# First batch of a Fourier-filter and MLP kernel: whole filter rows, units of four frequencies, the sign in the product, and three quarters of the last stages moved into the MLP

## The chip, the cores and the metric

The kernel runs on one core of one Trainium2 chip. The metric is the device time of one execution in microseconds (us). The kernel before takes 785.2 us (median of 3 runs, 785.15 to 785.42). Executions have two states, fast and slow.

Engines are named as the profile names them: PE is TensorE (matmuls), PEld its weight loads, DVE is VectorE, ACT is ScalarE, POOL is GpSimd, SP is SyncE (it issues transfers). L433 is line 433 of that kernel's file.

## The reference

```python
# x: 8 x 3008 x 256, filt_r and filt_i: 1505 x 256, w_in: 256 x 2048, w_out: 2048 x 256, beta: 2048
X = np.fft.rfft(x, axis=1)
y = np.fft.irfft(X * (filt_r + 1j * filt_i)[None], n=3008, axis=1)
h = y.reshape(24064, 256) @ w_in
g = h * (1.0 / (1.0 + np.exp(-beta * h)))
out = g @ w_out
```

## The kernel before

The Fourier filter is done as four matmul stages per batch element ("batch" below): stages 1 and 2 transform (3008 = 47 x 64), then comes the product with the filter, and stages 3 and 4 transform back. The MLP then runs over 47 blocks of 512 tokens in 16 steps each, 752 steps in all. A step is two matmuls into `hps`, one Silu on ScalarE from `hps` into `gT`, and four matmuls into `acc`.

Batch 0 is filtered before the MLP starts (the "setup"). Batches 1 to 7 are filtered inside the MLP, their instructions dealt out to its steps by a plan. The setup handles its product in six *units*. A unit is 8 of the 24 frequency groups and half of the 256 columns, so that a product on VectorE is 128x1024:

```python
parts = ((0, KH, 0, E2), (KH, 2 * KH, 0, E2), ...)      # KH = 8, E2 = 128: half rows, 512 bytes
def load_filters(k0, k1, d0, d1):
    for filt, dst, p0 in ((filt_r, fr_sb, 0), (filt_i, fi_sb, M)):        # M = 64
        for q0, off, sg in ((p0, k0, 1), (p0 + H, N1 - k0, -1)):          # H = 32 partitions each
            ...
            nc.sync.dma_start(dst[q0 : q0 + H, k0:k1, d0:d1], src)

def s2_0(n):                                   # stage 2 and the filter product of one unit
    ...
    for c, filt in enumerate((fr_sb, fi_sb)):
        r_t = p0pool.tile([P, KH, P], BF16, name="pq_t", tag=f"pq{c}")
        nc.vector.tensor_tensor(r_t[:], ps[:], filt[:, ks, ds], ALU.mult)

def spread(n):                                 # the second copy of the filter, in the other 64 partitions
    ...
    nc.gpsimd.tensor_copy(fr_sb[M:, ks, ds], fr_sb[:M, ks, ds])
    nc.gpsimd.tensor_copy(fi_sb[:M, ks, ds], fi_sb[M:, ks, ds])

# order on GpSimd: spread 0 to 4, load of w_in (1 MB), spread 5, loads of batch 1
```

Stage 3 used two tables, `t3` and a rotated copy `t3s` that carried the sign of the complex product. After it, TensorE turned (transposed) the result in 64 pieces (`z_turn`), stage 4 followed (`f_0`, `s4_0`), and all of that was done before the MLP. In the MLP the plan places the units of batch 1:

```python
s1_steps(1, range(16), [o + i // 2 for i in range(16)], False, range(1, 16, 2))
s23_steps(1, [o + r for r in (19, 21, 23, 26, 28, 30, 34, 36, 39, 41, 44, 46)], 5, 1)
```

A finished block leaves `acc` through two copies on VectorE into `ost`, queued two steps into the next block. `acc` has three buffers, and a block takes two.

## Time and profile before

| what | value | view |
|---|---|---|
| span of the profiled run | 782.8 us | head of the page |
| TensorE busy | 764.2 us, 98% | busy time by engine |
| TensorE busy from 60 to 120 us | 19.84 to 19.89 of each 20 us | busy time by stretches |
| first MLP matmul | 41.54 us | timeline of TensorE |
| products of the setup | 12, 1.14 us apart, 16.54 to 32.76 us | timeline of VectorE |

The busy time by engine on the page of the kernel before:

```profile
PE 764.2 (98%) x5978; PEld 544.9 (70%) x6071; DVE 438.1 (56%) x682; ACT 558.5 (71%) x824; POOL 151.6 (19%) x160
```

Busy time by stretches, kernel before (columns: stretch, its length, then busy time and instruction count of each engine, granted TensorE clock, DMA share, GB/s):

```profile
60.00:80.00 20.00, 19.89 (x144) 14.16 (x146) 16.83 (x25) 15.98 (x27) 9.55 (x10) 1.00 0.60 126
80.00:100.00 20.00, 19.84 (x140) 13.81 (x141) 13.22 (x20) 16.20 (x27) 7.62 (x6) 1.00 0.55 142
100.00:120.00 20.00, 19.84 (x159) 13.58 (x161) 11.81 (x19) 13.99 (x23) 1.54 (x3) 1.00 0.83 210
```

TensorE is the bound once the MLP runs. The setup is not bound by it: between 30 and 42 us it has gaps. Timeline of the kernel before (columns: start, duration, engine, line, operation, output<-inputs, shapes, and in brackets the idle time before it and what ended it), three lines of VectorE, then two of GpSimd and two of TensorE:

```profile
16.54 1.23 DVE L433 TENSOR_TENSOR pq_t<-sps,fr_sb 128x1024 bf16<-128x1024 f32 x1 [0.75 <-POOL fi_sb L468]
17.68 1.22 DVE L433 TENSOR_TENSOR pq_t<-sps,fi_sb 128x1024 bf16<-128x1024 f32 x1
...
31.55 1.21 DVE L433 TENSOR_TENSOR pq_t<-sps,fi_sb 128x1024 bf16<-128x1024 f32 x1
...
13.76 1.04 POOL L467 COPY fr_sb<-fr_sb 64x1024 f32<-64x1024 f32 x1 [3.18 <-DMA fr_sb<-in_filt_r_dram]
14.92 1.14 POOL L468 COPY fi_sb<-fi_sb 64x1024 f32<-64x1024 f32 x1
...
41.54 0.38 PE L756 MATMUL hps<-y,win_sb 128*128 128x512 bf16 x1 [0.43 <-ACT y L112]
42.30 0.39 PE L756 MATMUL hps<-y,win_sb 128*128 128x512 bf16 x1 [0.38 <-DVE y L116]
```

A unit of filter costs GpSimd two copies of about 1.04 us, and VectorE two products 1.14 us apart. GpSimd is thus as fast as VectorE. The transfers, kernel before, from 13 to 26 us (filter rows of 512 bytes), then from 26 to 28 us (the w_out loads, rows of 1 KB). The line that starts with q1 gives a queue's packets, MB, and the time that its packets took, as a share of 16 engines' time:

```profile
DMA packets 5817, 2.93 MB, mean 226 GB/s; under 512 B 336, under 2 KB 5816, under 8 KB 5816
...
DMA packets 665, 0.68 MB, mean 338 GB/s; under 512 B 15, under 2 KB 664, under 8 KB 664
...
q1 hardware_dynamic: 664, 0.66, 106.7%
```

### The profile page before, as it was taken

The page shows a single profiled execution, that of the slowest core. Times are in us where ns is not written, and L with a number is a line of the kernel's source. Part 1 is how long each engine was busy: PE and PEld are TensorE (multiplying, and loading weights), DVE is VectorE, ACT ScalarE, POOL GpSimd, SP SyncE. Part 2 cuts the span into 40 slices and gives each one's busy share as a digit, 9 for nine tenths or more (in the row PEclk, how much of TensorE's full clock was granted, in tenths as well). Part 3 has the DMA queues.
Part 4 walks back from the last instruction along what each step waited for, and adds up shares of the span by engine and source line. Part 5 has one row for each costly group of instructions (what it writes and reads, how often), then busy time and mean ns, then how long its engine had stood idle before and what let it go on. Part 6 is the DMA issues. An engine that isn't in the chain of part 4 may idle for free.

```text
span 782.8 us, 15166 instructions
## 1 busy us (share of the span) xinstructions
PE 764.2 (98%) x5978; PEld 544.9 (70%) x6071; DVE 438.1 (56%) x682; ACT 558.5 (71%) x824; POOL 151.6 (19%) x160
## 2 busy tenths in 40 slices
PE   8799999999999999999999999999999999999997
PEld 5666767766677667866678666786667776676665
DVE  7747654776556665566655675466655666320101
ACT  6788867676667766776667776677666777777776
POOL 6714300322012120122101222012200222000000
PEclk9999999999999999999999999999999999999999
DMA  9966675234822349033580416612164211500101
GB/s 178 230 190 138 145 201 167 68 88 120 238 75 64 98 114 260 32 84 99 121 236 29 126 56 158 198 58 85 49 188 118 66 48 49 155 28 28 55 28 55
DMA packets 89835, 88.51 MB, mean 113 GB/s; under 512 B 5708, under 2 KB 80972, under 8 KB 89764
## 3 DMA queue, kind: packets, MB, share of 16 engines
q1 hardware_dynamic: 85588, 73.81, 31.8%
q0 software_dynamic: 4032, 13.60, 10.5%
q8 instruction: 47, 0.77, 0.4%
q14 instruction: 24, 0.20, 0.1%
q10 hardware_dynamic: 144, 0.13, 0.1%
HBM read 54.47 MB, written 46.66 MB: 129 GB/s over the span
## 4 chain that ended last, share of the span: by engine, by line
PE 94%; ACT 2%; issue 1%; DVE 0%; ACTq 0%
PE acc L774 43%; PE hps L756 39%; PE ps L572 3%; PE ps L639 3%; PE ps L617 3%; PE ps L588 2%; ACT zT L112 1%; ACT zz L112 1%; ACT t3s L291 0%; DVE y L116 0%; PE sps L396 0%; PE sps L444 0%; PE tps L396 0%; ACT a L112 0%; PE sps L428 0%
## 5 line engine op out<-in xcount | busy, mean ns | idle before, releaser
L765 ACT ACTIVATE gT<-hps,beta_sb 128x512 bf16<-128x512 f32 x752 | 515.8, 687 | 208.3 <-PE hps L756 187.2
L774 PE MATMUL acc<-wout_sb,gT 128*128 128x256 bf16 x3008 | 453.2, 272 | 2.5
L756 PE MATMUL hps<-y,win_sb 128*128 128x512 bf16 (+7 forms) x1636 | 428.3, 350 | 1.1 <-ACT y L112 0.6
L774 PEld LDWEIGHTS <-gT 128*128 128x128 bf16 x3008 | 287.6, 98 | 125.9 <-issue 1.2
L607 POOL TENSOR_TENSOR yh<-a_t,b_t 128x512 bf16<-128x512 f32 x84 | 106.4, 1266 | 420.4 <-DVE b_t L606 419.5
L756 PEld LDWEIGHTS <-win_sb 128*128 128x128 bf16 x1728 | 164.9, 98 | 25.6 <-issue 0.7
L114 DVE COPY ost<-acc 128x512 f32<-128x512 f32 (+1 forms) x94 | 60.0, 679 | 147.1 <-PE acc L774 147.1
L114 DVE CAST a<-ps 96x512 bf16<-96x512 f32 x104 | 70.9, 685 | 52.1 <-PE ps L572 48.0
L602 DVE TENSOR_TENSOR a_t<-ps,fr_sb 128x512 f32<-128x512 f32 x84 | 58.1, 692 | 70.0 <-PE ps L588 69.5
L116 DVE TENSOR_SCALAR y<-ps 128x376 bf16<-128x376 f32 x104 | 56.0, 548 | 59.3 <-PE ps L639 59.1
L603 DVE SCALAR_TENSOR_TENSOR b_t<-ps,fi_sb 64x512 f32<-64x512 f32 x84 | 58.2, 692 | 1.1
L606 DVE TENSOR_TENSOR b_t<-ps,fi_sb 64x512 f32<-64x512 f32 x84 | 57.4, 683 | 1.1
L114 DVE CAST z<-ps 128x512 bf16<-128x512 f32 x72 | 49.3, 684 | 1.7 <-PE ps L617 0.8
L639 PEld LDWEIGHTS <-zz 96*128 96x128 bf16 x448 | 29.8, 98 | 22.9
L572 PE MATMUL ps<-xg,t 94*96 94x512 bf16 x112 | 41.5, 381 | 0.6
L639 PE MATMUL ps<-t,zz 96*128 96x94 bf16 x448 | 34.7, 205 | 0.8
L617 PE MATMUL ps<-yh,t 128*128 128x256 bf16 x168 | 32.1, 273 | 0.6
L588 PE MATMUL ps<-a,t 128*128 128x256 bf16 x168 | 32.1, 273 | 0.3
L617 PEld LDWEIGHTS <-t 128*128 128x128 bf16 x168 | 16.3, 98 | 17.7
L588 PEld LDWEIGHTS <-t 128*128 128x128 bf16 x168 | 16.1, 98 | 15.2
L171 POOL DMA_DIRECT2D xg<-in_x_dram x24 | 12.4, 519 | 56.5 <-PE ps L572 56.5
L572 PEld LDWEIGHTS <-t 94*96 94x96 bf16 x112 | 13.8, 123 | 10.3
(103 smaller groups left out, 185.9 us busy)
## 6 DMA issues: line engine op xcount, KB each, us to landing
out_dram<-ost SPq DMA_DIRECT2D x46, 512.0 KB, 3.0
d<-a SPq DMA_DIRECT2D x28, 384.0 KB, 4.7
a<-d SPq DMA_DIRECT2D x28, 384.0 KB, 5.1
d<-z SPq DMA_DIRECT2D x28, 384.0 KB, 3.7
zz<-d SPq DMA_DIRECT2D x28, 384.0 KB, 6.1
xg<-in_x_dram POOLq DMA_DIRECT2D x24, 384.0 KB, 6.2
ws<-in_moe_w_out_dram SPq DMA_DIRECT2D x4, 512.0 KB, 6.0
fr_sb<-in_filt_r_dram SPq DMA_DIRECT2D x12, 128.0 KB, 4.6
```

What stands on the lines that cost most here:

```text
L114: nc.vector.tensor_copy(dst, src)
L572: nc.tensor.matmul(ps[:KP], lhsT=t1[:], rhs=xg[b, g][:NP, jj : jj + 2, :], start=True, stop=True)
L588: nc.tensor.matmul(ps[:, e, :], lhsT=t2[:, k0 + e, :], rhs=st["a2", b, g][:, kk + e, :], start=True, stop=True,)
L602: nc.vector.tensor_tensor(a_t[:], ps[:], fr_sb[:, ks, :], ALU.mult)
L603: nc.vector.scalar_tensor_tensor(b_t[:M], ps[M:], -1.0, fi_sb[M:, ks, :], ALU.mult, ALU.mult)
L606: nc.vector.tensor_tensor(b_t[M:], ps[:M], fi_sb[M:, ks, :], ALU.mult)
L607: nc.gpsimd.tensor_tensor(yh[:], a_t[:], b_t[:], ALU.add)
L617: nc.tensor.matmul(ps[:, e, :], lhsT=t3[:, 2 * i + e, :], rhs=yh[:, e, :], start=True, stop=True)
L639: nc.tensor.matmul(ps[:, e, :NP], lhsT=zz[:, j0 % JG + e, dc * P : (dc + 1) * P], rhs=t4[:], start=True, stop=True,)
L756: nc.tensor.matmul(hps[:, pos - t0 : pos - t0 + ln], lhsT=win_sb[:, dc, fb * P : (fb + 1) * P], rhs=ys[b][:, dc, n0 : n0 + ln], start=(dc ...
L765: nc.scalar.activation(gT[:], hps[:], ACT.Silu, scale=beta_sb[:, fb : fb + 1])
L774: nc.tensor.matmul(acc_of(i, tb)[:, tb % 2, :], lhsT=blk[i * NFB + fb][:, tb * P : (tb + 1) * P], rhs=wout_sb[:, fb, :], start=(fb == 0 an ...
```

## The change

The intent: start the MLP earlier. Filter rows are loaded whole (1 KB instead of 512 bytes). A unit becomes 4 frequency groups and all 256 columns, still 128x1024. The sign goes into the second product, and into the copy of `fi_sb` that GpSimd makes, so that the second table shrinks to a 64-column negation. Only a quarter of the turns and of stage 4 of batch 0 stays before the MLP; the other three quarters, 48 turns and 48 matmuls, become planned work in its first 45 steps. To make room there, three of batch 1's twelve product units go to GpSimd, and the others move to later steps. The core of the diff:

```diff
-    def load_filters(k0, k1, d0, d1):
+    def load_filters(k0, k1):
         n = k1 - k0
-        for filt, dst, p0 in ((filt_r, fr_sb, 0), (filt_i, fi_sb, M)):
+        for filt, dst, p0 in ((filt_r, fr_sb, M), (filt_i, fi_sb, 0)):
...
-                nc.sync.dma_start(dst[q0 : q0 + H, k0:k1, d0:d1], src)
+                nc.sync.dma_start(dst[q0 : q0 + H, k0:k1, :], src)
...
-        for c, filt in enumerate((fr_sb, fi_sb)):
-            r_t = p0pool.tile([P, KH, P], BF16, name="pq_t", tag=f"pq{c}")
-            nc.vector.tensor_tensor(r_t[:], ps[:], filt[:, ks, ds], ALU.mult)
+        nc.vector.tensor_tensor(pq[u, 0][:], ps[:], fr_sb[:, ks, :], ALU.mult)
+        nc.vector.scalar_tensor_tensor(
+            pq[u, 1][:], ps[:], rot[:], fi_sb[:, ks, :], ALU.mult, ALU.mult
+        )
...
-        nc.gpsimd.tensor_copy(fr_sb[M:, ks, ds], fr_sb[:M, ks, ds])
-        nc.gpsimd.tensor_copy(fi_sb[:M, ks, ds], fi_sb[M:, ks, ds])
+        nc.gpsimd.tensor_copy(fr_sb[:M, ks, :], fr_sb[M:, ks, :])
+        nc.gpsimd.tensor_scalar_mul(fi_sb[M:, ks, :], fi_sb[:M, ks, :], -1.0)
...
+    for u in range(3):
+        spread(u)
+    nc.gpsimd.dma_start(win_sb[:], moe_w_in.rearrange("(dc p) f -> p dc f", p=P))
     spread(3)
+    spread(4)
+    load_x(1, 0)
+    spread(5)
...  # in the MLP's plan, batch 1
-            s1_steps(1, range(16), [o + i // 2 for i in range(16)], False, range(1, 16, 2))
+            at(0, z_late, 1, 0)
+            at(1, z_late, 1, 1)
+            s1_steps(1, range(16), [(2 * i + 1) // 3 for i in range(16)], False, (1, 4, 7, 10, 13))
+            for i, r in enumerate((11, 11, 12, 13)):
+                at(r, f_late, 1, i // 2, i % 2)
...
-            s23_steps(1, [o + r for r in (19, 21, 23, 26, 28, 30, 34, 36, 39, 41, 44, 46)], 5, 1)
+            for hh, z0, f0 in ((2, (14, 15), (16, 17, 18, 19)), (3, (20, 21), (23, 30, 37, 44))):
+                ...  # z_late and f_late of quarters 2 and 3
+            for i, r in enumerate((22, 25, 28, 29, 32, 35, 36, 39, 42, 43, 46, 49)):
+                pool_unit = i in (3, 6, 9)
+                at(o + r, s2, 1, i, pool_unit)
+                at(o + r + (8 if pool_unit else 5), s3, 1, i, True)
```

Left out: pools and tile shapes, the order of turns and stage 3 in the setup, the first four blocks stored in residue order (two transfers each), and one step less of delay at the very end.

## The prediction

> **What bounds the kernel now.** From about 44 to 779 us TensorE bounds everything: busy 19.8 to 19.9 of each 20 us (busy time by stretches), and in the waits after 44 us it waited 0.2 us for other engines. Before that, the first batch's setup is a latency chain with gaps on TensorE: the first MLP matmul starts at 41.54 us, the second at 42.30 us (timeline). In this chain VectorE runs twelve filter products, 1.14 us apart, from 16.54 to 32.76 us, with gaps and two table copies between; then 9 us go to the last back-transform, turns, last-stage matmuls and evacuations of all of batch 0.
>
> So the time is (start of the MLP) + (TensorE work after it) + a tail of about 4 us that the change hardly touches.
>
> **Removed, added, moved.**
> 1. Products: still twelve, 128x1024, at 1.14 us; the sign goes into the second (the sign form took 692 against 683 ns elsewhere). Rotations of the third table (4 x 0.6, 1.07 us) become smaller negations; the two 0.7 us copies on VectorE between the products move to ScalarE.
> 2. Filter loads: rows of 1 KB, not 512 B. The Trainium skill ("DMA: Bandwidth & Descriptors", Specifications) gives 512 B as enough for line rate. This trace differs: 226 GB/s while only 512 B packets move (13 to 26 us), 338 GB/s with 1 KB packets (26 to 28 us). A unit of filters then arrives in an estimated 1.6 us, not 2.3; GpSimd (2 x about 1.04 us a unit) paces instead, about as fast as VectorE.
> 3. The last stages before the MLP shrink to a quarter. My walk through the engine orders: first product at 16.0, a new gap of about 2 us on VectorE before the fourth product pair (two table turns stand ahead of its matmuls on TensorE and wait for ScalarE's evacuations), last product ending near 32, then 3 us of short evacuations: first MLP matmul near 35, 6 to 7 us earlier; 9 us if that gap does not occur.
> 4. Into the MLP go 48 turns (55 ns apart in the trace) and 48 last-stage matmuls (41.5 ns): 2.7 + 2.0 = 4.7 us of TensorE, at full price since TensorE is the bound there. VectorE stays at an estimated 44 of 57 us in the first 50 steps.
>
> **Sum.** Minus 7, plus 4.7, minus a few tenths for the ragged start: about 3 us less. Most of the earlier start is paid back as TensorE work.
>
> **Predicted: 782.3 us, 8 in 10 between 779.5 and 785.2.** Faster by over 2%: 0.01; within 2%: 0.97; slower by over 2%: 0.02.
>
> **What would show the steps.** Timeline: first MLP matmul at 34 to 36 us; last product ending at 31 to 33 us; the gap before the fourth pair. Stretches: filter packets of 1 KB above 300 GB/s. Groups: turn and last-stage matmuls at 55 and 41 ns spacing between 36 and 90 us. Waits after the start: TensorE idle under 1 us.
>
> **What would make it wrong.** GpSimd's negation of 64x1024 could cost more than a copy (two-input work of that length took 1.89 us) and pace the products: up to 2 us later. The weights or the next batch's rows could land late, as the DMA engines were saturated to 41 us before. VectorE could hold buffers in steps 11 to 25 and make TensorE wait. In the other direction, no gap at the fourth pair: about 780.

## The result, and the profile after

The kernel after takes 797.7 us (median of 4 runs, 797.32 to 798.05) beside 785.17 us for the kernel before (4 runs, 784.2 to 785.42). The ratio is 1.0162, 95% interval 1.0144 to 1.0179: 12.5 us slower. A ratio here is the mean time of one kernel's fast runs over that of the other's fast runs in the same rounds, so it is not quite the ratio of the medians. The interval lies wholly on the slow side, and the prediction's range (779.5 to 785.2) ends 12.5 us below it.

The first question is *where*. A table of when the MLP reaches a given step answers it. It lists the start of Silu number k in the timeline of ScalarE (us), counted from 0; the lines of step 56, before and after, stand below it:

| step | before | after | difference |
|---|---|---|---|
| 0 | 42.79 | 44.51 | +1.7 |
| 16 | 59.36 | 63.72 | +4.4 |
| 32 | 75.57 | 81.43 | +5.9 |
| 48 | 92.08 | 101.76 | +9.7 |
| 56 | 99.98 | 112.49 | +12.5 |
| 128 | 173.99 | 186.49 | +12.5 |
| 512 | 554.56 | 567.00 | +12.4 |

```profile
99.98 0.69 ACT L765 ACTIVATE gT<-hps,beta_sb 128x512 bf16<-128x512 f32 x1 [0.40 <-PE hps L756]
...
112.49 0.69 ACT L778 ACTIVATE gT<-hps,beta_sb 128x512 bf16<-128x512 f32 x1 [0.40 <-PE ps L555]
```

Everything is decided by step 56. The start is 1.7 us later instead of about 6.5 earlier, and the way from the first Silu to step 56 takes 67.98 us instead of 57.19: 10.8 us more, where 4.7 was expected.

The busy time by engine on the page of the kernel after. TensorE is busy only 3.4 us longer than before (767.6 against 764.2), part of it at half clock (below), so most of the 12.8 us by which the span grew (795.6 against 782.8) is TensorE waiting:

```profile
PE 767.6 (96%) x5952; PEld 545.9 (69%) x6046; DVE 443.4 (56%) x708; ACT 554.0 (70%) x814; POOL 172.4 (22%) x164
```

**The late start.** Timeline of the kernel after, GpSimd, then VectorE, then TensorE:

```profile
13.39 1.03 POOL L471 COPY fr_sb<-fr_sb 64x1024 f32<-64x1024 f32 x1 [4.23 <-DMA fr_sb<-in_filt_r_dram]
14.52 2.78 POOL L472 TENSOR_SCALAR fi_sb<-fi_sb 64x1024 f32<-64x1024 f32 x1
...
35.54 2.77 POOL L472 TENSOR_SCALAR fi_sb<-fi_sb 64x1024 f32<-64x1024 f32 x1
...
15.88 1.22 DVE L433 TENSOR_TENSOR pq_t<-sps,fr_sb 128x1024 bf16<-128x1024 f32 x1
...
38.34 1.28 DVE L434 SCALAR_TENSOR_TENSOR pq_t<-sps,rot,fi_sb 128x1024 bf16<-128x1024 f32 x1 [1.63 <-POOL fi_sb L472]
...
39.68 1.03 PE L443 MATMUL lp<-t,pq_t 128*128 128x128 bf16 x8 [1.87 <-DVE pq_t L434]
...
43.59 0.83 PE L769 MATMUL hps<-y,win_sb 128*128 128x512 bf16 x2
```

The first product starts at 15.88 us, as predicted (16.0). But the last one ends at 38.34 + 1.28 = 39.62 us, not near 32. GpSimd hardly pauses: each unit costs it 1.03 us for the copy and 2.77 us for the negation, where the kernel before paid two copies. What the trace says of `fi_sb` from 0 to 50 us in the kernel after (the operation's count and its shortest, median and longest duration in ns; then an entry of the list of who waited for this tile, with us and times):

```profile
L472 POOL TENSOR_SCALAR fi_sb<-fi_sb x6: 2763/2766/2783, 14.5 to 35.5; 64x1024 f32<-64x1024 f32 x6
...
  DVE pq_t L434: 8.1, 6
```

Each of the six second products waits for the negation, 8.1 us in all.

Between the late products TensorE has little to do, and its clock falls. Busy time by stretches, kernel after (the first figure after the stretch's length is TensorE's, the third from the end the granted clock):

```profile
30.00:32.00 2.00, 0.73 (x11) 0.71 (x12) 2.00 (x2) 0.08 (x1) 1.92 (x2) 1.00 1.09 221
32.00:34.00 2.00, 1.32 (x11) 0.88 (x9) 0.48 (x2) 0.95 (x1) 2.00 (x2) 0.67 0.45 90
...
40.00:42.00 2.00, 2.00 (x20) 1.79 (x19) 1.08 (x3) 0.93 (x3) 2.00 (x2) 0.50 0.81 158
```

So the last transforms before the MLP run at half clock. From the end of the last product to the first MLP matmul takes 43.59 - 39.62 = 3.97 us.

**The slow steps 24 to 56.** Busy time by stretches, kernel after, to be read against 19.84 in both stretches before:

```profile
80.00:100.00 20.00, 17.68 (x130) 12.13 (x130) 12.48 (x23) 14.14 (x23) 18.42 (x17) 1.00 0.53 116
100.00:120.00 20.00, 17.58 (x120) 11.81 (x120) 10.73 (x16) 13.06 (x22) 6.66 (x7) 1.00 0.48 127
```

The waits of TensorE, kernel after (us in total, times, longest); before, it had no wait for `ost` or `b_t` long enough to be listed:

```profile
PE acc L787 <- DVE ost L112: 3.1, 2, 2.3
...
PE ps L603 <- DVE b_t L591: 1.1, 3, 0.6
```

The longest of them in the timeline of the kernel after, first VectorE, then TensorE:

```profile
103.28 0.69 DVE L589 TENSOR_TENSOR a_t<-ps,fr_sb 128x512 f32<-128x512 f32 x1 [1.37 <-POOL yh L592]
...
105.40 1.29 DVE L112 COPY ost<-acc 128x512 f32<-128x512 f32 x2
...
106.14 0.38 PE L787 MATMUL acc<-wout_sb,gT 128*128 128x256 bf16 x2 [2.31 <-DVE ost L112]
```

The plan put a product unit at step 49, just before the copies that empty a finished block's `acc`. VectorE first waits 1.37 us for GpSimd to free a buffer, then works 2.1 us on the unit, and only then makes the copies for which TensorE stands.

**The filter loads.** Transfers of the kernel after, from 16 to 20 us:

```profile
DMA packets 709, 0.95 MB, mean 236 GB/s; under 512 B 116, under 2 KB 599, under 8 KB 709
...
q1 hardware_dynamic: 709, 0.95, 109.2%
```

Rows are 1 KB or more now, yet the rate is 236 GB/s, not the 338 that the prediction counted on. Some packets are longer still: in the forward half of each filter the rows of a unit's four groups lie next to each other in memory, and the packet records of the trace show 483 packets of 1 KB (72 ns each on average) and 110 of 4 KB (302 ns each) in this stretch. Per byte both take about as long.

### The profile page after: what moved, and what is told of

It reads as the page before. It is cut to its first block, busy times and chain, and to the rows that moved or that the text cites. A ratio compares the mean times of both kernels' runs of the same rounds, so it can differ in the third digit from the quotient of the medians.

```text
span 795.6 us, 15150 instructions
## 1 busy us (share of the span) xinstructions
PE 767.6 (96%) x5952; PEld 545.9 (69%) x6046; DVE 443.4 (56%) x708; ACT 554.0 (70%) x814; POOL 172.4 (22%) x164
## 4 chain that ended last, share of the span: by engine, by line
PE 85%; issue 1%; DVE 0%; ACT 0%; DVEq 0%; ACTq 0%
PE acc L787 40%; PE hps L769 36%; PE ps L555 3%; PE ps L625 3%; PE ps L603 2%; PE ps L571 2%; DVE ost L112 0%; ACT gT L778 0%; DVE b_t L591 0%; ACT y L110 0%; DVEq L823 0%; ACTq L778 0%
## 5 line engine op out<-in xcount | busy, mean ns | idle before, releaser
L112 DVE CAST a<-ps 96x512 bf16<-96x512 f32 x107 | 72.8, 685 | 52.4 <-PE ps L555 47.9
L589 DVE TENSOR_TENSOR a_t<-ps,fr_sb 128x512 f32<-128x512 f32 x81 | 56.0, 692 | 77.0 <-PE ps L571 70.6
L114 DVE TENSOR_SCALAR y<-ps 128x376 bf16<-128x376 f32 (+2 forms) x128 | 63.1, 510 | 60.9 <-PE ps L625 59.0
L590 DVE TENSOR_TENSOR b_t<-ps,fi_sb 64x512 f32<-64x512 f32 x81 | 56.1, 693 | 1.1
L591 DVE TENSOR_TENSOR b_t<-ps,fi_sb 64x512 f32<-64x512 f32 x81 | 55.3, 683 | 1.1
```

The costliest lines, as they stand in the source:

```text
L112: nc.vector.tensor_copy(dst, src)
L114: nc.vector.tensor_scalar_mul(dst, src, scale)
L589: eng.tensor_tensor(a_t[:], src[:], fr_sb[:, ks, :], ALU.mult)
L590: eng.tensor_tensor(b_t[:M], src[M:], fi_sb[M:, ks, :], ALU.mult)
```

## The experiments

The theories, by the letters that the expectations use: A, the negation on GpSimd paces the setup; B, the GpSimd units in the MLP make VectorE and then TensorE wait; C, the low clock makes the last part of the setup slow; D, the load of w_in makes the last filters late; E, transfers into 32 partitions are slow. Without a letter: the three quarters moved into the MLP cost more than they gain, and the order of instructions makes gaps. Twelve kernels were run, in four calls; each is compared with the kernel before in its own call (784.38, 784.41, 784.66 and, one run, 784.34 us).

### e1_copy: a copy in place of the negation

```diff
-        nc.gpsimd.tensor_scalar_mul(fi_sb[M:, ks, :], fi_sb[:M, ks, :], -1.0)
+        nc.gpsimd.tensor_copy(fi_sb[M:, ks, :], fi_sb[:M, ks, :])
```

The result is wrong (a sign is missing; relative error 0.999); nothing else changes.

> The changed kernel, but GpSimd copies the imaginary filters to the upper half instead of negating them (wrong sign in the result on purpose, same sizes and order everywhere). Theory A (the 2.77 us of the negation, against 1.03 us for a copy, paces the products and sets the start of the MLP): spreading falls from 3.9 to about 2.2 us a unit, the last product ends near 32 us instead of 39.6, the first MLP matmul comes near 35.5 instead of 43.6 us, the clock stays full in the setup, time about 797.7 - 8 = 789.5 us. Rival (the DMA landing of filters or the order of turns on TensorE paces as much): the start stays after 40 us and the time above 794.

Measured: 792.14 us (790.87 to 792.19), ratio 1.0096 (1.0081 to 1.0111). The first MLP matmul starts at 36.66 us, 6.9 us earlier than in the kernel after. Its timeline, GpSimd and TensorE, then its busy time from 100 to 120 us:

```profile
14.72 1.04 POOL L472 COPY fi_sb<-fi_sb 64x1024 f32<-64x1024 f32 x1
...
36.66 0.86 PE L769 MATMUL hps<-y,win_sb 128*128 128x512 bf16 x2
```

```profile
100.00:120.00 20.00, 20.00 (x133) 13.06 (x132) 8.57 (x14) 13.69 (x22) 1.06 (x2) 0.92 0.68 183
```

So theory A holds for the start: the operation kind alone moves it by 6.9 us. The span of the profiled run fell by only 5.2 us (795.6 to 790.4), because from the first Silu to step 56 this kernel took 69.65 us, 1.7 longer than the kernel after. The trouble in the MLP is thus a separate cause. It did not grow: TensorE's listed waits there are the same as in the kernel after (3.1 us for `ost`, 1.1 for `b_t`). But after the wait of 2.3 us for `ost` the granted clock stood at 0.50 from 99.6 to 103.0 us, and 3.4 us at half clock cost 1.7 us. The kernel after had the same wait and kept its clock at 1.00.

### e2_no_pool_units: no product unit on GpSimd

```diff
-                pool_unit = i in (3, 6, 9)
+                pool_unit = False
```

> The changed kernel, but no filter unit of the second batch goes to GpSimd: all twelve on VectorE, the third stage 5 steps later throughout. Theory B (the loss between 80 and 110 us comes from the three GpSimd units, 4 x 1.27 us each, which hold the output buffer and the product buffers): TensorE is busy 19.8 of each 20 us from 80 to 120 us instead of 17.6, time about 797.7 - 4.5 = 793 us. Rival (VectorE is overloaded there by the moved evacuations): giving VectorE three more units makes it worse or equal, 798 or more.

Measured: 796.23 us (795.72 to 796.73), ratio 1.0152 (1.0136 to 1.0167). From the first Silu to step 56: 66.13 us instead of 67.98, so 1.9 us are due to these units. TensorE still waits 2.6 us for `ost` (longest 1.9). Theory B is therefore a small part of it: the queue on VectorE by itself keeps `acc` waiting.

### e3_both: both, with a correct result

The negation goes back into the MLP's product, as before, and the setup's sign is adapted.

```diff
-    gp.tensor_tensor(rot[:], rot[:], affine("sgn", c_i, -2.0, 1.0, gp)[:], ALU.mult)
...
-        nc.gpsimd.tensor_scalar_mul(fi_sb[M:, ks, :], fi_sb[:M, ks, :], -1.0)
+        nc.gpsimd.tensor_copy(fi_sb[M:, ks, :], fi_sb[:M, ks, :])
...
-        eng.tensor_tensor(b_t[:M], src[M:], fi_sb[M:, ks, :], ALU.mult)
+        eng.scalar_tensor_tensor(
+            b_t[:M], src[M:], -1.0, fi_sb[M:, ks, :], ALU.mult, ALU.mult
+        )
...
-                pool_unit = i in (3, 6, 9)
+                pool_unit = False
```

> Both, with a right result: filters copied without the sign on GpSimd, the sign back in the scalar of the first batch's second product and in the later batches' sign form on VectorE; no units on GpSimd. If theories A and B are the whole of the miss and add up: about 797.7 - 8 - 4.5 = 785 us, and by my first sum 782.3. Rival (the two losses overlap, or another cost is hidden behind them): above 788.

Measured: 788.82 us (788.5 to 789.19), ratio 1.0057 (1.004 to 1.0073). Two thirds of the loss are gone, but it is still slower than before. Three lines of its timeline tell what is left (VectorE, GpSimd, TensorE):

```profile
26.54 1.23 DVE L432 TENSOR_TENSOR pq_t<-sps,fr_sb 128x1024 bf16<-128x1024 f32 x1 [1.59 <-PE sps L428]
...
31.77 1.04 POOL L471 COPY fi_sb<-fi_sb 64x1024 f32<-64x1024 f32 x1 [3.08 <-DMA fi_sb<-in_filt_i_dram]
...
98.02 0.38 PE L788 MATMUL acc<-wout_sb,gT 128*128 128x256 bf16 x2 [1.89 <-DVE ost L112]
```

First, the gap before the fourth product pair that the prediction foresaw, now visible: the pair before ends at 22.09 + 1.27 = 23.36 us, so it is 3.2 us (predicted about 2). Second, a new wait: the last part of the filter lands late. GpSimd, no longer slowed by the negations, issues the 1 MB load of w_in 3.2 us earlier than in the kernel after (21.91 instead of 25.13 us), and that load shares the DMA engines with the last filter loads. The negation had hidden this. Third, the wait for `ost` in the MLP is still there. This run also gives the price of the low clock: its clock is 1.00 from 28 us on, and from the last product's end (34.12 us) to the first MLP matmul (37.07 us) it takes 2.95 us, where the kernel after took 3.97. About 1.0 us of the late start is the clock.

### e4_clock_up: idle matmuls to hold the clock

Six idle matmuls before the second half of stage 3 of each of the last three units, added to the kernel after.

```diff
+            if c == 1 and u >= 3:
+                warm_up(u)
```

> The changed kernel with six idle 128x512 matmuls on TensorE in each of the last three waits for a second product, negation kept. Theory C (TensorE's gaps from 28 to 40 us let the granted clock fall to 0.5, and the last 10 us of the setup run at half speed): granted clock 1.0 throughout, the chain from the last product to the first MLP matmul falls from 4.0 to about 2.8 us, and the start ragged no more; time 1 to 2 us less, about 796. Rival: the clock does not matter, as GpSimd paces: same time within 0.3 us.

Measured: 800.13 us (798.68 to 802.26), ratio 1.0204 (1.0186 to 1.0221). It failed as an experiment. The last group of idle matmuls writes to a tile in a newly opened PSUM pool and itself waited 2.29 us until the last product, which reads the old pool, had ended; so it began when the real matmuls could have begun and held them back by 2.0 us. The clock fell all the same, to 0.50 from 42 to 44 us, and in this profiled run GpSimd also waited 1.56 us for the first imaginary filter part. The cost of the clock is therefore taken from e3_both, as above.

### e5_all_before: all last stages before the MLP again

From e3_both; all four quarters of the turns and of stage 4 run before the MLP. The plan of batch 1 stays that of the kernel after.

```diff
-    for e in range(NDC):
-        for h in range(2):
-            z_turn(0, e, 4 * h, 4, zps.tile([P, 4, P], BF16, name="zp", tag="zp"), h == 1)
+    for hh in range(HB):
+        for e in range(NDC):
+            for h in range(2):
+                z_turn(hh, e, 4 * h, 4, zps.tile([P, 4, P], BF16, name="zp", tag="zp"), h == 1)
...
-            at(0, z_late, 1, 0)
-            at(1, z_late, 1, 1)
...  # all other z_late and f_late removed
```

> The mended kernel (copy without sign, no GpSimd units), but with all four quarters of the first batch's last stages before the MLP, as the kernel before had them, and none inside it. My step of the prediction (the late work costs about 4.6 us of TensorE at full price, and sparing it before the MLP gains about 6 to 7 us of start): first gT near 44.5 us instead of 38.0, but the MLP's first 64 steps take about 8 us less (4.6 of work, 3.3 of TensorE's waits for VectorE); total about 787.5, within 2 us of the mended kernel. Rival (keeping work out of the MLP is simply better): 784 or less.

Measured: 788.85 us (787.86 to 789.09), ratio 1.0051 (1.0036 to 1.0066), level with e3_both. In the profile the first Silu comes 4.6 us later (42.63 against 38.01) and the way to step 56 is 6.2 us shorter (59.91 against 66.13). Moving these stages into the MLP is worth nothing. The wait for `ost` is unchanged to the hundredth, although no late stage is left, so it does not come from them:

```profile
96.41 0.38 PE L777 MATMUL acc<-wout_sb,gT 128*128 128x256 bf16 x2 [1.89 <-DVE ost L112]
```

### e7_two_input: the negation as a two-input product (one look)

```diff
-        nc.gpsimd.tensor_scalar_mul(fi_sb[M:, ks, :], fi_sb[:M, ks, :], -1.0)
+        nc.gpsimd.tensor_tensor(
+            fi_sb[M:, ks, :], fi_sb[:M, ks, :], minus[:M].unsqueeze(2).broadcast_to([M, KU, D]), ALU.mult
+        )
```

> The changed kernel with the negation written as a product of two inputs on GpSimd (the filters and a column of -1 spread over the row) instead of a product with a constant. If the operation kind sets the 2.77 us and not the shift of partitions, the size or the type: about 1.9 us, as the two-input product with the scales of the output weights (128x1024) has; products then paced at 3.0 instead of 3.9 us a unit, start near 39 us. If the shift of partitions[...] is what costs: 2.7 us or more again.

Measured: 792.59 us (a single run), correct. What the trace says of `fi_sb` in e7_two_input:

```profile
L475 POOL TENSOR_TENSOR fi_sb<-fi_sb,minus x6: 1888/1889/1890, 14.8 to 31.7; 64x1024 f32<-64x1024 f32 x6
```

The same negation costs 1.89 us with a tensor of -1 as second input and 2.77 us with a constant; a plain copy costs 1.03 us. The kind of operation sets the cost, not the data moved. The first Silu starts at 39.75 us, 4.8 us earlier than in the kernel after. Replacing one line by its slower-looking form is worth 4.8 us of the start.

### e8_reorder: the fourth pair's matmuls ahead of two turns

From e3_both.

```diff
+    s2_0(3)
     a0_turn(4)
+    unit(2)
     turn_t4()
     nc.vector.tensor_scalar(t4[0:4], t4[0:4], 0.5, None, ALU.mult)
     a0_turn(5)
-    s2_0(3)
-    unit(2)
```

> The mended kernel with the fourth unit's matmuls issued on TensorE ahead of the last two table turns. Theory: the gap of 3.1 us on VectorE before the fourth pair comes from this order, with the half clock that follows it; then the gap falls under 0.7 us, the clock stays full, first MLP matmul near 34.8 us instead of 37.1, time about 2.3 us less: 786.5. Rival (filters land too late, as the last imaginary part landed at 31.8 us): the start moves by under 0.7 us.

Measured: 789.48 us (788.09 to 789.89), ratio 1.0058 (1.0043 to 1.0073): no gain. The gap closed as meant, but the first MLP matmul stayed at 37.07 us. Two lines of its timeline, VectorE (the fourth pair) and GpSimd (the last filter part):

```profile
23.27 1.22 DVE L432 TENSOR_TENSOR pq_t<-sps,fr_sb 128x1024 bf16<-128x1024 f32 x1 [0.32 <-POOL fr_sb L470]
...
30.91 1.04 POOL L471 COPY fi_sb<-fi_sb 64x1024 f32<-64x1024 f32 x1 [3.03 <-DMA fi_sb<-in_filt_i_dram]
```

The rival was right: the last filter part, not the gap, ends the chain here. The last product did end 0.9 us earlier than in e3_both (33.26 against 34.12 us), but the granted clock was 0.50 from 34 to 36 us, and the way from there to the first MLP matmul took 3.81 us instead of 2.95.

### e9_relief: less work on VectorE in the MLP

From e8_reorder: the last quarter's evacuations go to ScalarE, and the product units move to steps that keep clear of the block ends.

```diff
-        f4_head(hh, h, e, ps, False)
-        f4_tail(hh, h, e, ps, False)
+        f4_head(hh, h, e, ps, on_act)
+        f4_tail(hh, h, e, ps, on_act)
...
-            for i, r in enumerate((22, 25, 28, 29, 32, 35, 36, 39, 42, 43, 46, 49)):
+            for i, r in enumerate((21, 23, 25, 28, 30, 32, 36, 38, 40, 42, 45, 47)):
```

> The reordered kernel, and inside the MLP: the last quarter's four late evacuations go to ScalarE, and the second batch's twelve filter units stand 1 to 3 steps earlier, in the rhythm of the kernel before, so none stands in VectorE's queue right ahead of a block's output copies. Theory (the waits of 3.3 us in steps 24 to 56 come from VectorE's queue ahead of those copies): TensorE's waits there fall under 0.8 us, time about 2.5 us less than the reordered kernel, 784. Rival (VectorE is simply too full, or the second batch's chain is short of time): waits stay above 2 us.

Measured: 788.42 us (786.0 to 789.41), ratio 1.0038 (1.0017 to 1.0059). The way from the first Silu to step 56 is 2.6 us shorter than in e8_reorder (63.95 against 66.53), and the wait for `ost` fell to 1.0 us. But the last filter part landed later still in the profiled run (its copy starts at 32.73 us), and the clock was 0.50 from 34 to 40 us, so the start was worse. The spread of 3.4 us between runs, larger than that of all other kernels but e4_clock_up (3.6), fits a wait whose end depends on how transfers mix; that is argued, not shown.

### e10_win_later: the w_in load two units later

From e9_relief.

```diff
-    nc.gpsimd.dma_start(win_sb[:], moe_w_in.rearrange("(dc p) f -> p dc f", p=P))
     spread(3)
     spread(4)
+    nc.gpsimd.dma_start(win_sb[:], moe_w_in.rearrange("(dc p) f -> p dc f", p=P))
     load_x(1, 0)
```

> The kernel of the last run (reordered, relieved MLP), with the load of the input weights issued on GpSimd after the fifth unit's filters are spread and not after the third's. Theory D (with the negation gone, GpSimd reaches the 1 MB load of the input weights some 4 us earlier, and it then shares the DMA engines with the last filters, which land at 31 to 33 us instead of 26): the last imaginary part lands before 28.5 us, the last product ends near 30.5 us, first gT near 35.5 us instead of 40.4 (38.1 in the run before that), step 56 of the MLP near 99.5 us (before: 100.0), time 784 or a little under. Rival (the filters land late by themselves): no change of the start.

Measured: 784.67 us (5 runs, 784.47 to 785.18), ratio 0.9997 (0.9985 to 1.001): level with the kernel before. Two lines of its timeline, GpSimd (the last part, now without a wait) and TensorE, then a line of its TensorE waits:

```profile
28.18 1.04 POOL L471 COPY fi_sb<-fi_sb 64x1024 f32<-64x1024 f32 x1
...
34.79 0.86 PE L770 MATMUL hps<-y,win_sb 128*128 128x512 bf16 x2
```

```profile
PE acc L788 <- DVE ost L112: 1.0, 1, 1.0
```

This is the start that the prediction promised (near 35 us). The first Silu comes 7.06 us earlier than before, and at step 56 the lead is 0.07 us: all of it has been paid back, since the way to step 56 takes 64.18 us instead of 57.19.

### e11_early_win_later: all last stages before the MLP, and the old plan

From e5_all_before, with the order of e8_reorder, the later w_in load, and the steps of batch 1's units as in the kernel before.

```diff
-            s1_steps(1, range(16), [(2 * i + 1) // 3 for i in range(16)], False, (1, 4, 7, 10, 13))
+            s1_steps(1, range(16), [o + i // 2 for i in range(16)], False, range(1, 16, 2))
...
-            for i, r in enumerate((22, 25, 28, 29, 32, 35, 36, 39, 42, 43, 46, 49)):
+            for i, r in enumerate((19, 21, 23, 26, 28, 30, 34, 36, 39, 41, 44, 46)):
```

> All last stages before the MLP, the reorder, the later load of the input weights, and for the second batch the plan of the kernel before in the MLP. What is left of the change: the whole filter rows, the units of 4, the sign in the product's scalar, the output in residue order. Theory: first gT near 40 us (before: 42.8), 57 to 58 us from there to step 56 as before, time near 782: faster than the kernel before by 2 to 3 us and than the last run by 2. Rival (the DMA engines or VectorE eat the gain elsewhere): 784 or more.

Measured: 783.69 us (5 runs, 783.21 to 783.86), ratio 0.9982 (0.9968 to 0.9996): the best of all, about 1 us better than the kernel before. The first MLP matmul in its timeline, and its busy time from 80 to 100 us:

```profile
40.33 0.38 PE L759 MATMUL hps<-y,win_sb 128*128 128x512 bf16 x1
```

```profile
80.00:100.00 20.00, 19.84 (x140) 13.81 (x141) 12.61 (x19) 16.38 (x26) 6.61 (x6) 1.00 0.50 130
```

TensorE is back at 19.84 of 20, and the way from the first Silu to step 56 takes 57.20 us, as before. The wait for `ost` is gone. Between e5_all_before and this kernel that way shrank by 2.7 us, and e5 had 2.6 us of waits for `ost` (two, 0.7 and 1.9): so that share belongs to the steps at which batch 1's work was planned. (The edit moved its units and also its stage 1 and two of its loads back to their old steps; the units alone were not tried.)

### e12_quarters: does the number of partitions set the rate? (one look)

From the kernel before: the w_out loads, 128 partitions each, are cut into four of 32 partitions, rows still 1 KB.

```diff
-        nc.sync.dma_start(
-            ws[:],
-            moe_w_out[f0 * P : (f0 + WG) * P, :].rearrange("(fb fp) j -> fp fb j", fp=P),
-        )
+        src = moe_w_out[f0 * P : (f0 + WG) * P, :].rearrange("(fb fp) j -> fp fb j", fp=P)
+        for q in range(4):
+            nc.sync.dma_start(ws[q * H : (q + 1) * H], src[q * H : (q + 1) * H])
```

> The kernel before, with each load of output weights (128 partitions, rows of 1 KB) cut into four DMAs of 32 partitions, rows and order of bytes the same. My step 2 said that the rows' length set the 226 against 338 GB/s; the changed kernel's 1 KB filter rows moved at 236. Theory E (a DMA into 32 partitions is what is slow): the stretch in which only these loads move falls from 338 to about 230 GB/s. Rival (the filters' source order, strides of 47 rows and reversed rows, is what is slow): it stays near 338. The time hardly moves in either case, under 1 us.

Measured: 784.84 us (a single run). Its transfers from 26 to 28 us, the stretch that showed 338 GB/s in the kernel before:

```profile
DMA packets 465, 0.41 MB, mean 207 GB/s; under 512 B 51, under 2 KB 465, under 8 KB 465
...
q1 hardware_dynamic: 465, 0.41, 110.7%
```

With the same row length the rate fell from 338 to 207 GB/s, as theory E expects. But the edit did two things: it also made four transfers of 128 KB out of one of 512 KB. SyncE took 4.75 us to issue the eight of them, 0.59 us each, which by itself would allow no more than 131 KB / 0.59 us = 221 GB/s.

### e13_slices: as many transfers, all of 128 partitions (one look)

From the kernel before: the same loads are cut into four of 128 KB again, but each writes all 128 partitions.

```diff
-        nc.sync.dma_start(
-            ws[:],
-            moe_w_out[f0 * P : (f0 + WG) * P, :].rearrange("(fb fp) j -> fp fb j", fp=P),
-        )
+        src = moe_w_out[f0 * P : (f0 + WG) * P, :].rearrange("(fb fp) j -> fp fb j", fp=P)
+        for q in range(WG):
+            nc.sync.dma_start(ws[:, q : q + 1], src[:, q : q + 1])
```

> The kernel before, with each of the two early w_out loads cut into four DMAs of 128 KB that write all 128 partitions (one block of 128 rows each, 1 KB rows). e12 cut them into four of 128 KB too, but of 32 partitions each, and fell from 338 to 207 GB/s between 26 and 28 us. That left two readings: the number of partitions, or the number of transfers (their issue took 4.75 us for 8, 0.59 us per 128 KB, which by itself allows only about 221 GB/s). If partitions set the rate, this run shows well over 300 GB/s once the filter loads are done, with issues of at most 0.4 us each; if the issue sets it, it shows about 200 to 230 GB/s as e12 did. The time should stay within 0.2% of the kernel before either way (784 to 786 us).

Measured: 784.23 us (a single run). Its transfers from 26 to 28 us:

```profile
DMA packets 423, 0.38 MB, mean 192 GB/s; under 512 B 45, under 2 KB 422, under 8 KB 422
...
q1 hardware_dynamic: 422, 0.38, 68.9%
```

The rate is low here too, so the rate of e12_quarters alone proves nothing: transfers of 128 KB, issued every 0.6 us, suffice to hold it down (8 issues took 4.82 us). What differs is how full the engines are. In e13_slices they are at 69%, starved by the issue; in e12_quarters they are full, at 111%, and yet move no more. Worked out from the q1 lines (share x 16 engines x 2 us / packets), a packet occupies an engine on average for 51 ns in the kernel before, 52 ns in e13_slices and 76 ns in e12_quarters. Counting the packets of 1 KB alone, the packet records give 52, 58 and 85 ns. Packets of the same length thus take about 1.5 times as long where a transfer writes 32 partitions. The filter loads write 32 partitions each, are 128 KB each, and keep the engines full (109% in the kernel after), so they look like e12_quarters and not like e13_slices. Their own packets agree: in the kernel after a filter packet of 1 KB took 72 ns (16 to 20 us), a w_out packet of 1 KB, into 128 partitions, 52 ns (26 to 28 us). No run changed the number of partitions of the filter loads themselves; for them the cause is an inference.

## Why the prediction was right or wrong

The prediction said 782.3 us; 797.7 was measured. Two of its steps failed: "GpSimd (2 x about 1.04 us a unit) paces" in step 2, since a negation takes 2.77 us and not 1.04, and "TensorE idle under 1 us" after the start, since the waits listed after 44 us are 4.9 us. Point by point:

**Step 1, the products: right.** There are twelve, 128x1024, the form with the sign takes 1.28 us against 1.22, and the first one starts at 15.88 us (predicted 16.0).

**Step 2, the filter loads: wrong, in its cause and in "GpSimd (2 x about 1.04 us a unit) paces instead".** There are two errors in it. The larger one: a negation was costed as a copy. It takes 2.77 us, and there are six of them, so a unit costs GpSimd 3.8 us instead of 2.1, and the last product ends at 39.62 us, not near 32. The risk was named, with the two-input duration of 1.89 us as its size and "up to 2 us later" as its worth. The trace of the kernel before had this kind of operation on GpSimd only on tiny tiles (4x94 took 0.47 us, 128x16 0.29 us), so the size was guessed from another kind. The prediction passed over what the Trainium skill says ("GPSIMD Engine Reference", 4.1 Engine selection): two-input operations are about two times slower on GpSimd than on VectorE, one-input ones run roughly at line rate. This roughly agrees for the copy (1.03 us) and the two-input product (1.89 us, where VectorE took 1.22 us for a two-input product with rows of the same length), and differs for the one-input product with a constant (2.77 us). The measurement decides. With e1_copy the first MLP matmul moves from 43.59 to 36.66 us: 6.9 of the 8.6 us between 43.59 and the predicted 35, of which about 1.0 is the fallen clock.

The second error: "338 GB/s with 1 KB packets" was read as an effect of row length. Rows at least doubled in the kernel after, and the rate went from 226 to 236 GB/s only. What e12_quarters and e13_slices show in its place are two other limits on the w_out loads: packets into 32 partitions hold an engine 1.5 times as long, and transfers of 128 KB, issued every 0.6 us, allow no more than about 220 GB/s. The second is not the limit of the filter loads: they are 128 KB each too, but SyncE issued them every 0.45 to 0.57 us, and the engines were full. The Trainium skill states the first ("SBUF — State Buffer", Door 1: The DMA port swizzle): the bandwidth depends on how many of 16 ports the partitions reach, 32 partitions reach 8 of them, and its asymptote for 8 ports is about 218 GB/s. The numbers here are near it: 207 GB/s in e12_quarters, 226 and 236 for the filter loads; no run shows why the last two lie above it. The prediction set the page "DMA: Bandwidth & Descriptors" (Specifications: 512 B suffice for line rate) against the trace and said that they differ. No run here shows that they do, since the limit was another. As to time this error cost little: in e10_win_later, with the copy in place, no product waits more than 0.33 us for GpSimd.

**Step 3, the start: right to a few tenths, once two waits are removed, and in part by luck.** The gap before the fourth pair exists (3.2 us against about 2 predicted), "first MLP matmul near 35" is 34.79 in e10_win_later. But that kernel no longer has this gap, and for that case the prediction promised 9 us, a start near 32.5. In e10_win_later VectorE instead stood 1.0 us before the fifth pair and 0.33 us before the fourth, and the last product ended at 31.84 us. Only the 3 us from there to the first MLP matmul (2.95) came out as said. The kernel after missed it because of the negation, and behind the negation stood a second cause that was named only in general ("the weights ... could land late"): it was not the weights that landed late, but the last filter part, because the weights were loaded beside it. With the copy in place, removing this wait and the gap together moved the first MLP matmul from 37.07 to 34.79 us (e3_both to e10_win_later); removing the gap alone moved nothing (e8_reorder), since the late filter part and the half clock took its place.

**Step 4, the late stages: their TensorE price was right, but "TensorE idle under 1 us" failed, since "VectorE stays at an estimated 44 of 57 us" does not guard against waits.** The 48 turns and 48 matmuls cost what was said: 8 turns take 0.44 us and 4 matmuls 0.165 us in the timeline, so 48/8 x 0.44 + 48/4 x 0.165 = 4.6 us. VectorE's load was even lower than estimated, 39.1 of the 57.3 us from the first Silu to step 48. But an average load says nothing about the order of the work: TensorE waited 3.1 us for `ost`, 1.1 for `b_t` and 0.7 for others. The 10.8 us by which the way to step 56 grew divide like this:

| part | us | from |
|---|---|---|
| late turns and stage 4, TensorE work | 4.6 | durations in the timeline |
| the rest of what the late stages cost | 1.6 | e3_both to e5_all_before (6.2), less 4.6 |
| batch 1's work planned at other steps, units just ahead of a block's copies | 2.7 | e5_all_before to e11_early_win_later |
| three product units on GpSimd | 1.9 | kernel after to e2_no_pool_units |
| sum | 10.8 | |

The split holds for this order of removal; the 1.7 us that e1_copy lost on top were the half clock from 99.6 to 103.0 us, which is no part of it. Of the 1.6 us, 0.7 may be waits for `b_t`, which e3_both has and e5_all_before has not; the rest was not settled.

**The sum.** Predicted: start 7 us earlier, 4.7 paid back. Measured in the kernel after: start 1.7 us later (first Silu), 10.8 paid. Even with these faults removed, but for a wait of 1.0 us for `ost`, the move does not pay: between e11_early_win_later and e10_win_later the first MLP matmul comes 5.5 us earlier (40.33 against 34.79), and the way to step 56 takes 7.0 us longer (64.18 against 57.20). At best, with no wait at all, an estimated 5.5 - 4.6 = 0.9 us could be won, because TensorE, the bound of the MLP, has to do that work either way. What pays is in the rest: e11_early_win_later, with whole rows, units of four, the sign in the product, the output in residue order, and the mended order of the setup, beats the kernel before by about 1 us. Which of these parts gives it was not tested. Its lead at step 64 was 1.75 us in the profile; the rest went in the tail, which was not looked into.

## What to carry to other kernels

Cost a new operation by its exact kind on its engine, from a trace that has this kind; when the trace has none, the error can exceed the cost itself (here 2.77 us against an assumed 1.04), and the range has to be as wide. Moving work out of a latency chain into a stage whose bound is the same engine only shifts the time: compare the time saved in the chain with the time added to the bound before anything else. When work is dealt out to steps, look at what stands in each queue ahead of the instruction that frees a buffer of the bounding engine, because an average load of an engine hides a wait of 2 us behind one badly placed unit. Before a run's extra loss is given a new cause, look at the granted clock of its stretches: in e1_copy it explained all of it.

## What the Trainium skill lacked or had wrong

- "GPSIMD Engine Reference" (4.1 Engine selection) calls one-input operations on GpSimd roughly line-rate. Here a copy of 64x1024 f32 took 1.03 us, but a product of the same tile with a constant took 2.77 us, more than the two-input product of the same tile (1.89 us, e7_two_input). The page would need to tell copies from one-input arithmetic.
- "TensorE: Matmul & The Clock Gate" (Why this matters for your kernels) advises no idle gaps over about 3 us between bursts. In the kernel after, the granted clock fell from 1.00 to 0.50 at about 32.7 us though the longest stretch without a matmul before that was 2.3 us (28.97 to 31.27 us). So keeping to the advice is not enough; in e3_both the clock fell too (0.63 from 24 to 26 us), after a longest stretch of 1.6 us. Nor does the same stretch always lower it: in e5_all_before TensorE was busy only 0.20 of the 2 us from 22 to 24 us, with a stretch of 1.6 us too, and the clock stayed at 1.00. The page does say elsewhere that frequent short idle times can lower the clock, but no page gives a threshold for the share of work, and no run here measured one.
- "SBUF — State Buffer" (Door 1: The DMA port swizzle) has the rule that explains the long packets, and the runs agree with it (85 ns a packet of 1 KB into 32 partitions in e12_quarters, 52 and 58 ns into 128 in the kernel before and e13_slices). "DMA: Bandwidth & Descriptors" gives in its Specifications only the length (512 B) as the condition for line rate; its advice of 128 partitions and large transfers stands only in later sections, and a reference from the Specifications to the ports might have prevented the prediction's error. It gives no time measured on trn2 for the issue of a transfer by SyncE: in e13_slices transfers of 128 KB were issued every 0.6 us and left the engines at 69%, at 192 GB/s, where transfers of 512 KB had reached 338.
